# Linear attention plus a gated GLU on one core: interleaved two-sign features, transposes moved to DMA, key-value sums kept in PSUM

## The chip, the cores and the metric

The kernel runs on one core of one Trainium2 chip. The metric is the device time of one execution in microseconds (us), less being better. Spans in the profile run from the first to the last instruction and are 1 to 2 us shorter than the times. The kernel before was run in the same rounds on the same chip each time.

The engines are TensorE (PE in the profile, with PEld for its weight loads), VectorE (DVE), ScalarE (ACT), GpSimd (POOL) and SyncE (SP), which issues most of the DMA transfers. A q after an engine's name (SPq, DVEq) means its queue issuing, not working. PSUM is the memory that TensorE writes its results to; the program uses it as eight banks of 512 columns.

## The reference, cut to what matters

```python
B, S, D, H, Dh, F = 1, 2048, 512, 32, 16, 1792
xn  = layernorm(x)
q, k, v = split(xn @ wqkv)                       # 32 heads of 16
pq, pk  = q @ w_phi, k @ w_phi                   # 16x16 per head
phi_q = concat([softmax(pq), softmax(-pq)])      # 32 features per head
phi_k = concat([softmax(pk), softmax(-pk)])
kv  = einsum("sf,sd->fd", phi_k, v);  z = phi_k.sum(s)      # per head
o   = (phi_q @ kv) / (phi_q @ z + 1e-6)
out = x + o @ wo + ((xn @ w_gate) * (xn @ w_up)) @ w_down
```

Inputs and outputs are bfloat16. There are 16 tiles of 128 tokens.

## The kernel before

`w_phi` is folded into the key and query weights at the start. Each of the 16 token tiles then passes a key stage; after the key-value sums, a query stage. The positive and the negative features lie in two separate tiles. The parts that the change touches are these (all cut).

The loads: all of x, then the attention weights, then the rest, each as one large transfer.

```python
for g in range(4):
    sc.dma(SP, <x tiles 4g..4g+3>, ...)
for w in range(2):
    sc.dma(SP, wqk_v[:, w, :, :], ...)           # query, then key weights
sc.dma(SP, wv_v, ...); sc.dma(SP, wo_v, ...); sc.dma(SP, wg_v, ...); ...
```

The key-value sums come after all key tiles, with a column of ones beside each group of eight heads (129 columns):

```python
for g in range(8):
    pairs = [(ek_v[:, side, t, c*128:(c+1)*128], vext_all[:, t, c, :]) for t in range(NT)]
    mm_group(bank(b, lo, 129), pairs)
```

In the query stage TensorE transposes the features (eight 128x128 blocks per tile), makes numerators (128 columns, most of them masked to zero) and denominators (8 columns) with separate matmuls, and transposes the output (four blocks). ScalarE empties each transpose from PSUM.

```python
for side in range(2):
    items = [(bank(tb[side], c*128, 128), src[:, c*128:(c+1)*128], ident) for c in range(NQ)]
    mm_multi(items)
    act_op(eT_all[:, r, side*4:(side+1)*4, :], bank(tb[side])..., func=ACTF.Copy)
for c in range(NQ): mm_group(bank(bo, c*128, 128), <2 pairs with kvbd>)
for c in range(NQ): mm_group(bank(tb[0], c*8, 8),  <2 pairs with zbd>)
...
mm_multi(<4 transposes of oring>); act_op(oT_v[...], ...)
```

The GLU is done in two ways: 5 of the 14 feature tiles early, in units of 512 tokens; 9 late, in halves of 256 columns, inside the output stage. The residual x is added on TensorE, by a matmul of x with the identity (`acc_mm(i, ident, x_tile(t))`).

The softmax here doesn't subtract the row's maximum and nothing guards it: scores larger than these inputs give would overflow.

Of the kernel before, what the change touches and what calls it, by code (L numbers as in the profile page):

```python
# [5 lines left out]
BF16 = mybir.dt.bfloat16  # L6
# [4 lines left out]
I32 = mybir.dt.int32  # L11
# [6 lines left out]
DH = 16  # L18
# [4 lines left out]
FT_EARLY = 5  # L23


def _ap_intervals(ap, max_n=64):
    esz = mybir.dt.size(ap.dtype)
    off = ap.offset
    pairs = [tuple(pr) for pr in list(ap.ap)[1:] if pr[1] > 1]
    inner_hi = 0  # L30
    rest = []
    for step, cnt in pairs:
        if step == 1:
            inner_hi = max(inner_hi, cnt - 1)
        else:
            rest.append((step, cnt))
    total = 1
    for step, cnt in rest:
        total *= cnt
    if total > max_n:  # L40
        lo, hi = 0, inner_hi
        for step, cnt in rest:
            if step > 0:
                hi += step * (cnt - 1)
            else:
                lo += step * (cnt - 1)
        return [((off + lo) * esz, (off + hi + 1) * esz)]
    outs = []
    for n in range(total):
        base = off  # L50
        m = n
        for step, cnt in rest:
            base += step * (m % cnt)
            m //= cnt
        outs.append((base * esz, (base + inner_hi + 1) * esz))
    return outs


class _Step:
# [3 lines left out]
    def __init__(self, eng, fn, idx, lane):  # L63
        self.eng = eng
        self.fn = fn
        self.idx = idx
        self.deps = []
        self.sig = False
        self.lane = lane
        self.semval = None  # L70
        self.known = {}
        self.waits = []
        self.is_out = False
        self.cost = 100.0
        self.seq = 0
        self.finish = 0.0


class _Sched:

    def __init__(self, nc):
        self.nc = nc
        self.steps = []
        self.by_eng = {PE: [], ACT: [], DVE: [], POOL: [], SP: []}
        self.regions = {}
        self.dma_count = 0
        self.allow_overwrite = False

    def _overlaps(self, space, lo, hi):
        out = []  # L90
        for reg in self.regions.setdefault(space, []):
            if reg[0] < hi and lo < reg[1]:
                out.append(reg)
        return out

    def _record(self, st, reads, writes):
        deps = []
        for ap in reads:
            space = str(ap.tensor.name)
            ivs = _ap_intervals(ap)  # L100
            if space == "ps":
                ivs = sorted(set((lo // 2048 * 2048, (hi + 2047) // 2048 * 2048) for lo, hi in ivs))
            for lo, hi in ivs:
                regs = self._overlaps(space, lo, hi)
                for reg in regs:
                    if reg[2] is not None and reg[2] is not st:
                        deps.append(reg[2])
                    reg[3].append(st)
                if not regs:
                    self.regions[space].append([lo, hi, None, [st]])  # L110
        for ap in writes:
            space = str(ap.tensor.name)
            for lo, hi in _ap_intervals(ap):
                new_regions = []
                for reg in self._overlaps(space, lo, hi):
                    if reg[2] is not None and reg[2] is not st and not reg[3] and not self.allow_overwrite:
                        raise RuntimeError(
                            f"step {st.idx} ({st.eng}) overwrites unread data in {space}[{reg[0]}:{reg[1]}] "
                            f"written by step {reg[2].idx} ({reg[2].eng})")
                    if reg[2] is not None and reg[2] is not st:  # L120
                        deps.append(reg[2])
                    for r in reg[3]:
                        if r is not st:
                            deps.append(r)
                    if reg[0] < lo:
                        new_regions.append([reg[0], lo, reg[2], list(reg[3])])
                    if reg[1] > hi:
                        new_regions.append([hi, reg[1], reg[2], list(reg[3])])
                    self.regions[space].remove(reg)
                self.regions[space].extend(new_regions)  # L130
                self.regions[space].append([lo, hi, st, []])
        seen = set()
        dd = []
        for d in deps:
            if id(d) not in seen:
                seen.add(id(d))
                dd.append(d)
        st.deps = dd

    def step(self, eng, fn, reads=(), writes=(), cost=None):  # L140
        st = _Step(eng, fn, len(self.steps), eng)
        self.steps.append(st)
        self.by_eng[eng].append(st)
        reads = list(reads)
        writes = list(writes)
        self._record(st, reads, writes)
        if cost is None:
            n = 1
            for ap in writes + reads:
                try:  # L150
                    n = max(n, ap.free_size())
                except Exception:
                    pass
            if eng == ACT:
                cost = 230.0 + 0.84 * n
            elif eng == DVE:
                cost = 130.0 + 1.0 * n
            elif eng == POOL:
                cost = 250.0 + 2.2 * n
            else:  # L160
                cost = 100.0 + 0.45 * n
        st.cost = cost
        return st

    def dma(self, eng, out_ap, in_ap, is_out=False, reads=None, writes=None):
        nc = self.nc
        lane = ("dma", self.dma_count)
        self.dma_count += 1
        holder = {}

        def fn(e):
            ins = e.dma_start(out_ap, in_ap)
            return ins

        st = _Step(eng, fn, len(self.steps), lane)
        st.sig = True
        try:
            nbytes = out_ap.free_size() * 2 * 128
        except Exception:
            nbytes = 131072  # L180
        st.cost = 2000.0 + nbytes / 300.0
        self.steps.append(st)
        self.by_eng[eng].append(st)
        r = list(reads) if reads is not None else ([in_ap] if str(in_ap.tensor.name).startswith(("arena", "ps")) else [])
        w = list(writes) if writes is not None else ([out_ap] if str(out_ap.tensor.name).startswith(("arena", "ps")) else [])
        self._record(st, r, w)
        st.is_out = is_out
        return st

# [18 lines left out]
def _build(nc, es, A_x, A_wqkv, A_w_phi, A_wo, B_w_gate, B_w_up, B_w_down, out):  # L208
# [3 lines left out]
    def alloc(name, nelem_bf16, at=None):  # L212
        if at is not None:
            layout[name] = at
            return at
        off = (cur[0] + 31) // 32 * 32
        layout[name] = off
        cur[0] = off + nelem_bf16
        return off

    alloc("x", NT * 512)
    alloc("xnT", NQ * S_TOK)
    alloc("xn", 4 * 512)
    o_wqk = alloc("wqk", 2 * NQ * 512)
    alloc("wT", 2 * NQ * 512)
# [5 lines left out]
    alloc("wd", NF * 512)  # L231
    alloc("wphi", NQ * 16)
# [3 lines left out]
    alloc("bind8", 8)  # L236
    alloc("vext", NT * NQ * 129)
    o_ek = alloc("ek", 2 * NT * 512)
    alloc("ering", 6 * 512, at=o_wqk)
    alloc("enr", 3 * 512, at=o_wqk + 3072)  # L240
    alloc("eT", 2 * 8 * 128, at=o_wqk + 4608)
    alloc("kvbd", 8 * 128, at=o_wqk + 6656)
    alloc("zbd", 8 * 8, at=o_wqk + 7680)
    alloc("oT", NQ * S_TOK, at=o_ek)
    alloc("oring", 3 * 512)
    alloc("gring", 3 * 512)
    alloc("hring", 3 * 512)
    alloc("hT", FT_EARLY * S_TOK)
    alloc("ostg", 3 * 512)
    alloc("stats", 2 * NT * 8)  # L250
    alloc("mv", 2 * NT * 2)
    alloc("rstd", 2 * NT * 2)
    alloc("sums", 2 * 6 * 64)
    alloc("rs", 2 * 6 * 64)
    alloc("small", 2 * 6 * 64)
    alloc("eps", 2 * 2)
    alloc("lnt", 2 * 3 * NT)
    alloc("zcol", 2 * 8 * 2)
    total_bf16 = (cur[0] + 31) // 32 * 32
    assert total_bf16 * 2 <= 207 * 1024, f"arena too big: {total_bf16*2}"  # L260

    arena_t = es.enter_context(nc.sbuf_tensor("arena", [128, total_bf16], BF16))
    arena = arena_t[:, :]
    psum_t = es.enter_context(nc.psum_tensor("ps", [128, 8 * 512], F32))
    psum = psum_t[:, :]

    def sbv(name, lo, n):
# [3 lines left out]
    def sbf(name, lo_f32, n_f32):  # L271
        off = layout[name]
        return arena[:, off:off + 2 * (lo_f32 + n_f32)].bitcast(F32)[:, lo_f32:lo_f32 + n_f32]

    def bank(b, lo=0, n=512):
        return psum[:, b * 512 + lo: b * 512 + lo + n]

    sc = _Sched(nc)
# [658 lines left out]
```

## Time and profile before

The median was 271.5 us of 3 runs (270.5 to 272.2). Only TensorE is near its limit:

| engine | busy us of 270.5 | share |
|---|---|---|
| TensorE matmuls | 246.2 | 91% |
| VectorE | 156.2 | 58% |
| ScalarE | 128.1 | 47% |
| GpSimd | 53.8 | 20% |

The page's second part cuts the span into 40 slices; a digit is the busy share in tenths. Its PE row and the shares of the chain that ended last, from the page of the kernel before:

```profile
PE   0068999999999999999999999999999999999994
PE 80%; DVE 8%; ACT 3%; DMA 3%; issue 3%; POOL 2%; DVEq 0%; POOLq 0%
```

TensorE is full (9) from the fifth slice to the last but one. So the question for any change is how much time its matmuls need and when they begin. Three pieces of the chain in order of time (start us, us, what) were my sources for the cost of one matmul:

```profile
64.39 10.74 PE ps L309 x49
94.65 7.29 PE ps L309 x103
121.61 1.52 PE ps L309 x24
```

Divided they give 0.219, 0.071 and 0.063 us per matmul.

TensorE's start, from the timeline of the kernel before (start us, us, engine, line, operation, shapes, count, and in brackets the idle time before and its releaser):

```profile
14.89 1.04 PE L323 MATMUL ps<-arena 128*128 128x128 bf16 x8 [14.89 <-POOL arena L450]
16.28 1.07 PE L323 MATMUL ps<-arena 128*128 128x128 bf16 x8 [0.35 <-ACT arena L287]
18.04 1.04 PE L323 MATMUL ps<-arena 128*128 128x128 bf16 x8 [0.69 <-ACT arena L287]
```

TensorE has nothing before 14.89 us. The releaser named is POOL, but the weight load that goes with this matmul waits for the transfer of the qkv weights.

### The profile page before, as it was taken

The numbers are of one execution on the slowest core, as the hardware profiler recorded it, in microseconds if no ns is written. First come the engines' busy times: TensorE is split into PE (matmuls) and PEld (weight loads), VectorE is DVE, ScalarE is ACT, GpSimd is POOL, SyncE is SP. The second block draws the span as 40 slices with busy tenths as digits, with TensorE's granted clock in tenths as the row PEclk, the third lists the DMA queues.
The fourth block names the chain that finished last, engine by engine and source line by source line (L and its number), as shares of the span: only waits on it lengthen the run. The fifth ranks groups of instructions, "written<-read, shape, count | busy, mean of one in ns | idle before, by whom it ended". The sixth has DMA issues, their size and how long they took to land.

```text
span 270.5 us, 4879 instructions
## 1 busy us (share of the span) xinstructions
PE 246.2 (91%) x1902; PEld 156.7 (58%) x1936; DVE 156.2 (58%) x364; ACT 128.1 (47%) x261; POOL 53.8 (20%) x99
## 2 busy tenths in 40 slices
PE   0068999999999999999999999999999999999994
PEld 0046544444444587777567765775766757566661
DVE  3951699989797985787677776542232323313231
ACT  1057898646665704776665755632222313222221
POOL 4560253333442430313112131100000000000000
PEclk9999999999999999999999999999999999999999
DMA  6999300000000000000000001001001010000101
GB/s 198 351 393 381 119 0 1 2 0 0 0 0 2 0 4 2 0 2 0 22 19 2 4 1 41 0 2 39 0 2 39 2 39 0 26 15 2 39 1 39
DMA packets 9446, 12.12 MB, mean 45 GB/s; under 512 B 448, under 2 KB 8400, under 8 KB 9424
## 3 DMA queue, kind: packets, MB, share of 16 engines
q1 hardware_dynamic: 9392, 11.80, 12.6%
q8 instruction: 15, 0.25, 0.4%
q0 software_dynamic: 32, 0.02, 0.1%
q14 instruction: 7, 0.06, 0.1%
HBM read 9.72 MB, written 2.10 MB: 44 GB/s over the span
## 4 chain that ended last, share of the span: by engine, by line
PE 80%; DVE 8%; ACT 3%; DMA 3%; issue 3%; POOL 2%; DVEq 0%; POOLq 0%
PE ps L309 50%; PE ps L654 24%; PE ps L323 7%; ACT arena L287 3%; DMA arena<-in_A_w_phi_dram 3%; DVE arena L499 2%; DVE arena L506 1%; DVE arena L534 1%; DVE arena L504 1%; POOL arena L395 1%; DVE arena L465 1%; DVE arena L576 0%; DVE arena L679 0%; DVE arena L457 0%; POOL arena L449 0%
## 5 line engine op out<-in xcount | busy, mean ns | idle before, releaser
L287 ACT ACTIVATE arena<-ps 128x512 bf16<-128x512 f32 (+1 forms) x260 | 126.9, 541 | 138.9 <-PE ps L309 92.9
L309 PE MATMUL ps<-arena 128*128 128x256 bf16 (+4 forms) x1300 | 172.6, 279 | 1.6 <-ACT arena L287 0.5
L309 PEld LDWEIGHTS ps<-arena 128*128 128x128 bf16 x1312 | 109.0, 98 | 59.0 <-PE ps L309 2.2
L654 PE MATMUL ps<-arena 128*128 128x512 bf16 x282 | 77.9, 381 | 2.0 <-DVE arena L679 0.6
L679 DVE TENSOR_TENSOR arena<-ps,arena 128x256 bf16<-128x256 f32 x72 | 30.0, 416 | 55.3 <-PE ps L654 52.9
L323 PE MATMUL ps<-arena 128*128 128x128 bf16 x320 | 30.9, 240 | 17.6 <-POOL arena L450 14.9
L654 PEld LDWEIGHTS ps<-arena 128*128 128x128 bf16 x304 | 28.0, 97 | 24.4 <-PE ps L654 4.4
L323 PEld LDWEIGHTS ps<-arena 128*128 128x128 bf16 x320 | 24.4, 107 | 27.1 <-DMA arena<-in_A_wqkv_dram 14.9
L506 POOL TENSOR_TENSOR arena<-arena 128x512 bf16<-128x512 bf16 x16 | 22.6, 1413 | 34.6 <-DVE arena L504 26.3
L584 POOL TENSOR_TENSOR arena<-arena 128x512 bf16<-128x512 bf16 x16 | 16.9, 1056 | 63.0 <-DVE arena L582 47.0
L576 DVE TENSOR_REDUCE arena<-arena 128x32 f32<-128x512 bf16 x32 | 20.6, 678 | 7.3 <-ACT arena L287 7.2
L499 DVE TENSOR_REDUCE arena<-arena 128x32 f32<-128x512 bf16 x32 | 20.6, 678 | 6.0 <-ACT arena L287 6.0
L534 DVE TENSOR_TENSOR arena<-ps,arena 128x512 bf16<-128x512 f32 x20 | 13.6, 682 | 1.5 <-PE ps L309 1.4
L432 DVE BATCH_NORM_STATS2 arena<-arena 128x6 f32<-128x512 bf16 x16 | 10.5, 684 | 4.8 <-DMA arena<-in_A_x_dram 4.8
L707 DVE CAST arena<-ps 128x512 bf16<-128x512 f32 x8 | 5.5, 692 | 12.4 <-PE ps L654 12.3
L506 DVE TENSOR_TENSOR arena<-arena 128x512 bf16<-128x512 bf16 x16 | 11.6, 728 | 0.4
L465 DVE TENSOR_SCALAR arena<-arena 128x512 bf16<-128x512 bf16 x16 | 5.8, 410 | 9.8 <-PE ps L323 9.8
L621 DVE TENSOR_TENSOR arena<-ps,arena 128x512 bf16<-128x512 f32 x16 | 10.9, 682 | 0.3
L504 DVE RECIPROCAL arena<-arena 128x64 f32<-128x64 f32 x16 | 8.8, 550 | 0.4
L618 DVE SCALAR_TENSOR_TENSOR arena<-arena,ps 128x32 f32<-128x32 f32 x16 | 3.0, 188 | 10.3 <-PE ps L309 10.1
L620 DVE RECIPROCAL arena<-arena 128x32 f32<-128x32 f32 x16 | 5.6, 351 | 0.4
L581 DVE RECIPROCAL arena<-arena 128x32 f32<-128x32 f32 x16 | 5.6, 348 | 0.4
(31 smaller groups left out, 30.3 us busy)
## 6 DMA issues: line engine op xcount, KB each, us to landing
arena<-in_A_x_dram SPq DMA_DIRECT2D x4, 512.0 KB, 6.6
out_dram<-arena SPq DMA_DIRECT2D x16, 128.0 KB, 1.7
arena<-in_B_w_gate_dram SPq DMA_DIRECT2D x1, 1792.0 KB, 12.0
arena<-in_B_w_up_dram SPq DMA_DIRECT2D x1, 1792.0 KB, 15.2
arena<-in_B_w_down_dram SPq DMA_DIRECT2D x1, 1792.0 KB, 18.1
arena<-in_A_wqkv_dram SPq DMA_DIRECT2D x3, 512.0 KB, 11.2
arena<-in_A_wo_dram SPq DMA_DIRECT2D x1, 512.0 KB, 8.9
arena<-in_A_w_phi_dram POOLq DMA_DIRECT2D x1, 16.0 KB, 7.5
```

The source lines that it names most:

```text
L287: return e.activation(out=out_ap, in_=in_ap, func=func, scale=scale, **kw)
L309: ins = e.matmul(out_ap, lhsT=l, rhs=r, start=(i == 0), stop=(i == n - 1))
L323: ins = e.matmul(o, lhsT=l, rhs=r, start=True, stop=True)
L499: dve(lambda e, side=side: e.tensor_reduce(out=sm[:, side * 32:(side + 1) * 32], in_=ering(slot, side).rearrange("p (h f) -> p h f", f=16) ...
L504: dve(lambda e: e.reciprocal(out=rs, in_=sm), [sm], [rs])
L506: fn = (lambda e, side=side: e.tensor_tensor(out=ek_v[:, side, t, :].rearrange("p (h f) -> p h f", f=16), in0=ering(slot, side).rearrange( ...
L534: dve(lambda e: e.tensor_tensor(out=dest_ap, in0=bank(bu), in1=gring(slot), op=ALU.mult), [bank(bu), gring(slot)], [dest_ap])
L576: dve(lambda e, side=side: e.tensor_reduce(out=sm[:, side * 32:(side + 1) * 32], in_=ering(slot, side).rearrange("p (h f) -> p h f", f=16) ...
L584: pool(lambda e: e.tensor_tensor(out=enr(slot).rearrange("p (h f) -> p h f", f=16), in0=ering(slot, 1).rearrange("p (h f) -> p h f", f=16) ...
L621: dve(lambda e: e.tensor_tensor(out=oring(slot).rearrange("p (h d) -> p h d", d=16), in0=bank(bo).rearrange("p (h d) -> p h d", d=16), in1 ...
L654: return e.matmul(o, lhsT=lhsT, rhs=rhs, start=first, stop=last)
L679: dve(lambda e: e.tensor_tensor(out=h, in0=bank(bu, 256, 256), in1=g, op=ALU.mult), [bank(bu, 256, 256), g], [h])
```

## The change

The intent is to take from TensorE all that is not a product of the model. The program is largely rewritten; the diff below is cut to its core and cuts are marked.

```diff
-    <transposes of q features on PE, evacuated by ACT>          # 8 per tile
+    def q_transpose(t):
+        sc.dma(SP, lambda e: e.dma_start_transpose(ph_tile(t), src), ...)       # 256 KB
-    <transposes of o on PE, evacuated by ACT>                   # 4 per tile
+        sc.dma(SP, lambda e: e.dma_start_transpose(oT_tile(t), o_tile(t)), ...) # 128 KB
...
+    # features token-major [token, head, sign, 16]: 4 heads = 128 columns with both signs
+    e_v = sb(name, s*1024, 1024).rearrange("p (h k f) -> p h k f", h=H, k=2)
+    act(e_v[:, :, 0, :], src, func=Exp); act(e_v[:, :, 1, :], src, func=Exp, scale=-1.0)
...
+    # v is scaled by 1/sum; column 17 of each head is 1/sum itself: z comes with kv
+    def kv_acc(t):                       # two tiles after the features, into PSUM banks 0 and 1
+        for c in range(8):
+            e.matmul(bank(c//4, (c%4)*68, 68), lhsT=ek[:, c*128:(c+1)*128], rhs=vs[:, c*68:(c+1)*68],
+                     start=(t == 0 and c % 4 == 0), stop=(t == NT-1))
-    <8 numerator matmuls of 128 columns, 8 denominator matmuls of 8 columns per tile>
+    <8 matmuls of 68 columns per tile: 4 heads x (16 numerators + 1 denominator)>
...
-    <GLU: 5 feature tiles in 512 columns, 9 in 256 columns>
+    <GLU: all 14 feature tiles in 512 columns, spread over the key and query stages>
-    acc_mm(i, ident, x_tile(t))                          # residual on PE
+    dve(lambda e: e.tensor_tensor(out=stg, in0=bank(b), in1=x_tile(t), op=ALU.add), ...)
...
-    <loads: x, query, key, value, wo, gate, up, down>
+    <loads: x 0-1, key, x 2-3, value, gate/up in slices of 256 columns mixed with the rest of x, ...>
-    <1/sqrt of the layernorm by Newton steps on POOL>
+    <by Ln and Exp on ACT>
```

## The prediction

> **What bounds the kernel now.** TensorE. In the busy table PE is busy 246.2 of 270.5 us, in the forty slices it is at 9 from the third to the last, and 80% of the chain that ended last is PE. A sum of issue spacings, read from the timeline, reproduces the span: 644 matmuls of 512 columns at 0.219 us (49 in 10.74 us) = 141; 576 of 256 columns at 0.111 = 64; 576 small ones of 128 or 8 columns at about 0.064 = 37; 128 of 129 columns at 0.071 = 9. Together 251 us. PE starts at 14.9 us (it waits for the qkv weights, loaded after all of x) and the output tail takes 3 us: 269.
>
> **What the change removes, adds, moves.**
> - The 256-column GLU halves become 512-column units: 64 us become 63.
> - Removed from PE: 128 q-feature and 64 output transposes (12 us), 128 denominator matmuls (8 us; the denominator is now column 17 of each head), 16 residual matmuls (3.5 us). Key-value sums and numerators use 68 columns instead of 129 and 128: about 1 us, as weight loads hold these near 0.064.
> - After: 928 matmuls of 512 columns = 203 us, 384 small ones = 25 us: 228, that is 23 us less, all on the critical path because PE is saturated.
> - ACT loses the evacuations of these transposes and of v (64 ops of 0.6 us). DVE gains the v multiply and 8 more residual ops, loses the ek multiply (0.73x16).
> - Start: the key weights are second in the queue, so PE should begin near 6 us. Transposing and folding them is paced by ACT evacuations (0.6 us each, 12 of them), so PE is dense from about 13.5 us, having done 3 of the 228 us. Before, it was dense only near 24 us, having done about 6.
> - Moved to DMA: 32 transposing copies, 256 and 128 KB per token tile, on the queue of SP. No trace here shows one. The Trainium skill, "Advanced Engine Details and Errata", X-Bar Transpose (TRN2), says they run as fast as ordinary ones, about 350-400 GB/s. Then a tile needs 1 us of transfer plus fixed latency, with a lead of three tiles (a tile of the query stage takes 8.8 us of PE with GLU units, 5.3 without). That is hidden.
>
> **New costs.** In the first six key iterations DVE has about 6.3 us (two layernorm tiles 2.3, reduction 1.2, reciprocal 0.55, multiplies 2.2) against PE 6.3 us, with only two PSUM banks for features, v and x transposes: I expect 4 us of PE gaps there and at the boundaries.
>
> **Sum.** 13.5 + 225 + 4 + 3.2 = 246 us; 8 in 10 between 238 and 264. Chances: faster by over 2% 0.86, within 2% 0.05, slower 0.09.
>
> **What would show it.** PE busy near 228; first dense PE at 12 to 15 us; transposing DMAs landing in under 5 us; in the query stage no PE wait on a DMA; gaps of PE in 14 to 55 us released by DVE or ACT; 512-column matmuls still spaced 0.219.
>
> **What would make it wrong.** Slow transposing DMAs. The skill's page "VectorE: DVE Perf Modes", The three transpose paths, gives 1309 ns for one 128x128 block; if that is a rate and not a latency, twelve blocks take 16 us per tile, the query stage is bound by DMA and the kernel is slower than before. The first eight are also chained by completion waits on SP. Second: DVE queue order in the key stage starving the two shared banks, 10 us more.

The 1 us of transfer per tile in it is an estimate worked out from the rate of the page that it names; no run measured that rate.

## The result, and the profile after

The changed kernel took 237.8 us (median of 4 runs, 237.4 to 239.4); the kernel before 271.7 us in the same rounds. The ratio of the fast runs is 0.876, 95% interval 0.871 to 0.880. The forecast, 246 us with a range of 238 to 264, had the direction right and was too cautious: the result lies just below the range.

The lines of the page after that answer to those of before:

```profile
PE   0897959999999999999999999999999999999994
PE 88%; SPq 4%; DVE 3%; DMA 3%; issue 1%
```

TensorE begins earlier, is not full in slices 4 and 6, and is then full to the last but one. The pieces of the chain in the query stage after (line 206 is all 512-column matmuls, line 454 the numerators of 68 columns):

```profile
199.98 3.45 PE ps L206 x16
203.43 0.26 PE ps L454 x8
203.69 4.75 PE ps L206 x22
```

These pieces hold one shape each, so they may be divided: 0.216 us per 512-column matmul and 0.0325 us per 68-column one. The second number is half of what the prediction had charged.

**The cost of a matmul, measured properly.** Taking the start of each single matmul from the recorded trace, and the median distance to the next start after 30 us, gives:

```
columns          8     68    128    129    256    512
ns to the next   25    31.5   56     56    109    216      (before: 8, 128, 129, 256, 512; after: 68, 128, 512)
```

This agrees with the Trainium skill, "TensorE: Matmul & The Clock Gate", Wait — 56ns, not 53.3ns?, which gives N/2.4 GHz plus about 2.5 ns and a floor near 25 ns. The distance is set by the columns, although every matmul here has its own weight load of about 98 ns (the mean of PEld's large groups, both kernels). The loads overlap the matmuls and each other: around the eight 68-column matmuls at 203.27 us they start 30 to 35 ns apart and take 95 to 101 ns each.

**The ledger of the gain.** With these distances the work of TensorE is (the counts are of the program; 34 of 1,936 matmuls are missing from the trace of before, as its weight loads show):

| columns | before | us | after | us |
|---|---|---|---|---|
| 512 | 656 | 141.7 | 928 | 200.4 |
| 256 | 576 | 62.8 | 0 | 0 |
| 128, 129 | 576 | 32.3 | 128 | 7.2 |
| 68 | 0 | 0 | 256 | 8.1 |
| 8 | 128 | 3.2 | 0 | 0 |
| sum | | 240.0 | | 215.7 |

The spans went from 270.5 to 235.7 us, 34.8 us less. Of that, 24.3 us are matmul work. TensorE's first matmul comes 9.2 us earlier (5.7 against 14.9). The rest, idle and slow time of TensorE and the tail, is almost the same in both (about 1 us less).

**What is left at the start.** The timeline of TensorE after, a selection:

```profile
5.72 1.04 PE L309 MATMUL ps<-arena 128*128 128x128 bf16 x8 [5.72 <-POOL arena L287]
...
14.46 3.75 PE L206 MATMUL ps<-arena 128*128 128x512 bf16 x10 [0.22 <-issue]
19.73 0.40 PE L356 MATMUL ps<-arena 128*128 128x128 bf16 x4 [1.52 <-DVE arena L346]
19.97 1.89 PE L206 MATMUL ps<-arena 128*128 128x512 bf16 x8
...
32.66 0.40 PE L356 MATMUL ps<-arena 128*128 128x128 bf16 x4 [2.36 <-DVE arena L346]
32.90 2.75 PE L206 MATMUL ps<-arena 128*128 128x512 bf16 x12
```

Two losses show. Two gaps, before 19.73 and 32.66 us, end when VectorE has normalised a tile of x (line 346). And ten matmuls of 512 columns took 3.75 us at 14.46, though eight took 1.89 us at 19.97. Start to start, the first group is 427 ns apart until 17.4 us, about twice the 216 ns (the shown durations have a tail of some 0.17 us at the end of a group). This is the half rate of a TensorE that has not been busy for long enough (same page, Part 1: The HAM clock gate; it gives some 3.4 us of sustained activity). The trace agrees where TensorE has no pause: in the run with 120 idle matmuls (experiment 7) they are 107 ns apart from 1.85 us on and 56 ns apart from 5.03 us, 3.2 us later. In the control's trace TensorE's idle and slow time, over the distances of the table, is about 11 us between first and last matmul, all of it before 33 us; after that no matmul waits.

The copies that replaced the transposes land 3.1 us after issue (median of 32) and no wait of TensorE on them is in the list of waits.

### The profile page after: what moved, and what is told of

Same layout as the page of the kernel before. It is cut to its first block, busy times and chain, and to the rows that moved or that the text cites. A ratio compares the mean times of both kernels' runs of the same rounds, so it can differ in the third digit from the quotient of the medians.

```text
span 235.7 us, 3357 instructions
## 1 busy us (share of the span) xinstructions
PE 220.7 (94%) x1287; PEld 107.6 (46%) x1312; DVE 146.1 (62%) x282; ACT 87.4 (37%) x165; POOL 42.8 (18%) x65
## 4 chain that ended last, share of the span: by engine, by line
PE 88%; SPq 4%; DVE 3%; DMA 3%; issue 1%
PE ps L206 82%; SPq L238 3%; DMA arena<-in_A_x_dram 3%; PE ps L454 2%; PE ps L413 2%; PE ps L356 1%; DVE arena L337 1%; DVE arena L488 1%; SPq L227 1%; DVE arena L382 0%; PE ps L309 0%; PE ps L320 0%; DVE arena L378 0%; DVE arena L503 0%; DVE arena L346 0%
## 5 line engine op out<-in xcount | busy, mean ns | idle before, releaser
L206 PE MATMUL ps<-arena 128*128 128x512 bf16 x903 | 206.6, 381 | 1.5 <-issue 0.2
L206 PEld LDWEIGHTS ps<-arena 128*128 128x128 bf16 x928 | 88.3, 98 | 100.7 <-issue 2.4
L187 ACT ACTIVATE arena<-ps 128x512 bf16<-128x512 f32 (+1 forms) x152 | 84.5, 597 | 117.2 <-PE ps L206 103.3
L378 DVE TENSOR_REDUCE arena<-arena 128x64 f32<-128x1024 bf16 x32 | 38.9, 1216 | 32.8 <-ACT arena L187 32.8
L388 POOL TENSOR_TENSOR arena<-arena 128x512 bf16<-128x512 bf16 x32 | 34.0, 1061 | 90.6 <-DVE arena L386 86.1
L488 DVE TENSOR_TENSOR arena<-ps,arena 128x512 bf16<-128x512 f32 x56 | 38.4, 686 | 11.9 <-PE ps L206 11.7
L503 DVE TENSOR_TENSOR arena<-ps,arena 128x512 bf16<-128x512 f32 x16 | 11.1, 691 | 30.0 <-PE ps L206 30.0
L400 POOL CAST arena<-arena 128x32 bf16<-128x32 f32 x16 | 5.2, 326 | 77.5 <-DVE arena L382 74.1
L466 DVE TENSOR_TENSOR arena<-ps,arena 128x512 bf16<-128x512 f32 x16 | 11.1, 692 | 0.6
L356 PE MATMUL ps<-arena 128*128 128x128 bf16 x64 | 7.0, 240 | 4.3 <-DVE arena L346 3.9
L401 DVE TENSOR_TENSOR arena<-ps,arena 128x512 bf16<-128x512 f32 x16 | 10.2, 635 | 0.1
L309 PE MATMUL ps<-arena 128*128 128x128 bf16 x32 | 3.8, 264 | 6.0 <-POOL arena L287 5.7
L356 PEld LDWEIGHTS ps<-arena 128*128 128x128 bf16 x64 | 4.9, 105 | 8.6 <-DVE arena L346 4.9
L454 PEld LDWEIGHTS ps<-arena 128*128 128x128 bf16 x128 | 6.2, 97 | 3.8
L413 PEld LDWEIGHTS ps<-arena 128*128 128x128 bf16 x128 | 5.8, 97 | 1.9
L454 PE MATMUL ps<-arena 128*128 128x68 bf16 x128 | 6.7, 194 | 0.0
L413 PE MATMUL ps<-arena 128*128 128x68 bf16 x128 | 6.7, 194 | 0.0
L309 PEld LDWEIGHTS ps<-arena 128*128 128x128 bf16 x32 | 2.7, 117 | 7.4 <-DMA arena<-in_A_wqkv_dram 5.7
L386 DVE TENSOR_TENSOR arena<-arena 128x32 f32<-128x32 f32 x32 | 5.9, 184 | 0.2
## 6 DMA issues: line engine op xcount, KB each, us to landing
arena<-in_A_wo_dram SPq DMA_DIRECT2D x1, 512.0 KB, 11.6
```

Source lines behind the costliest of these rows:

```text
L187: return sc.step(ACT, lambda e: e.activation(out=out_ap, in_=in_ap, func=func, scale=scale, **kw), reads, writes, 130.0 + 0.833 * n)
L206: ins = e.matmul(out_ap, lhsT=l, rhs=r, start=start and i == 0, stop=stop and i == npair - 1, **kw)
L356: ins = e.transpose(bank16(b, q * 128, 128), xn_tile(t)[:, q * 128:(q + 1) * 128], ident)
L378: dve(lambda e: e.tensor_reduce(out=sm, in_=e_v, axis=AX.X, op=ALU.add), [(name, s, 0), (name, s, 1)], [("sums", sr)], 1024)
L388: pool(lambda e: e.tensor_tensor(out=e_v[:, :, 1, :], in0=e_v[:, :, 1, :], in1=rat[:, :, None].to_broadcast([128, H, 16]), op=ALU.mult), [ ...
L401: dve(lambda e: e.tensor_tensor(out=vs_tile(t)[:, :, 0:16], in0=bank(b).rearrange("p (h f) -> p h f", h=H), in1=rp.unsqueeze(2).to_broadca ...
```

## The experiments

There were 17 runs besides the first. They ask whether the terms of the ledger are real (1 to 4), whether the copies through DMA are free (5), and what the early start is worth (6 and 7). Everywhere below the ratio is to the kernel before of the same rounds. The changed kernel itself, repeated as a control, gave 0.877 (237.7 us) and in the last set, on another chip, 0.880 (239.0 us).

### 1. Control

No edit.

> The changed kernel unaltered, as the control of this set. All theories: 237 to 239 us. Spacing of its 256 matmuls of 68 columns, start to start, again about 31 ns.

Measured: 237.67 us, ratio 0.877, span 235.7 us. Spans here and below are those of the profiled execution. The 256 matmuls of 68 columns are again 31.5 ns apart.

### 2. Columns or weight loads

```diff
-            ins = e.matmul(bank(c // 4, (c % 4) * CW, CW), ..., rhs=vs[:, c * CW:(c + 1) * CW], ...)
+            ins = e.matmul(bank(c // 4, (c % 4) * 128, 128), ..., rhs=vs[:, c * CW:c * CW + 128], ...)
```

The numerators likewise; the outputs are stored 128 columns apart and the extra 60 are ignored.

> The 256 key-value and numerator matmuls stream 128 columns (68 useful, 60 ignored) instead of 68. Theory W (the recorded prediction: weight loads hold a small matmul near 64 ns, whatever its columns): spacing and time unchanged, within 1 us. Theory C (columns set the spacing[...]): spacing goes from 31 to 56 ns, 256 x 0.025 = 6.3 us longer, about 244 us.

Measured: 244.8 us, ratio 0.902, span 242.1 us, which is 6.4 us over the control's. The spacing rose to 56 ns. The same place of the timeline in the control, then in this run (columns as above):

```profile
203.29 0.42 PE L454 MATMUL ps<-arena 128*128 128x68 bf16 x8
203.54 2.75 PE L206 MATMUL ps<-arena 128*128 128x512 bf16 x12
```

```profile
203.55 0.61 PE L462 MATMUL ps<-arena 128*128 128x128 bf16 x8
204.00 2.32 PE L208 MATMUL ps<-arena 128*128 128x512 bf16 x10
```

From the start of the eight to the start of what follows it is 0.25 us against 0.45. Theory C holds and the prediction's claim about weight loads falls. Packing numerator and denominator into 68 columns is worth all of its columns.

### 3. The transposes back on TensorE

```diff
-        sc.dma(SP, lambda e: e.dma_start_transpose(ph_tile(t), src), ...)
+        <8 e.transpose into a PSUM bank>; act(ph_tile(t), <bank>, ...)
-        sc.dma(SP, lambda e: e.dma_start_transpose(oT_tile(t), o_tile(t)), ...)
+        <4 e.transpose into the same bank>; act(oT_tile(t), <bank>, ...)
```

> Both transposes of the query stage go back to TensorE (192 transposing matmuls of 128 columns), evacuated by ScalarE. Theory C: TensorE is without gaps there, so the time grows by 192 x 0.056 = 10.8 us, to about 248.5 us. The recorded prediction (64 ns each) says 12.3 us. Rival: the transposes fall into gaps that the copies through DMA had left, or ScalarE's 32 more evacuations make new waits: growth under 6 us or over 15 us.

Measured: 262.2 us, ratio 0.966, span 258.6 us: 22.9 us over the control, far more than the 10.7 us of matmuls. The gaps have a name, in the timeline of this run:

```profile
211.97 0.61 PE L445 MATMUL ps<-arena 128*128 128x128 bf16 x8
212.51 0.42 PE L462 MATMUL ps<-arena 128*128 128x68 bf16 x8
214.32 0.40 PE L485 MATMUL ps<-arena 128*128 128x128 bf16 x4 [1.39 <-ACT arena L187]
```

The transposes of the output (485) wait for ScalarE to empty the bank that the feature transposes (445) had filled. My placement made that wait, so a second version gives them separate banks once the GLU units, which hold four of the eight banks, are done:

```diff
-        b = 2 if ups else 3        # o_transpose
+        b = 2 if ups else 7
-        b = 3 if ups else 4 + i % 4
+        b = 3 if ups else 4 + i % 3
```

> As e_petr, but once the GLU units are done the two transposes use separate PSUM banks (3 and 7) and the output tiles three banks. e_petr grew by 22.9 us of span: 10.7 us of matmuls and 12.3 us of TensorE gaps, 8.9 of them after 190 us, where an output transpose waits for ScalarE to empty the same bank. Theory (the transposes themselves cost only their 10.7 us, the rest was bank sharing): span about 250 us, time about 252 us. Rival (ScalarE's 32 evacuations are themselves the limit): no change from e_petr's 262 us.

Measured: 254.5 us, ratio 0.936, span 252.9 us, 17.2 us over the control. TensorE's gaps after 190 us fell from 8.9 to about 1 us, as the theory said. Those at 119 to 144 us (3.5 us), where the GLU units still hold their banks, stayed. Some 2 us of the 17.2 are not the transposes': this execution fell to half rate from 20.1 to 23.5 us, after a gap at the start that the control has too. The one run at full granted clock has a span of 251.0 us, 15.3 over the control's and 1 us over the forecast. So moving the transposes to DMA saves 10.7 us of matmuls, and in this schedule also waits for PSUM banks and ScalarE's emptying, another 4.6 us. How many of those a third placement would recover is open.

### 4. The residual back on TensorE

```diff
-        mm(bank(b), [(oT_tile(t)[:, q, :], wo_v[:, q, :]) for q in range(NQ)], ...)
+        mm(bank(b), [(oT_tile(t)[:, q, :], wo_v[:, q, :]) for q in range(NQ)] + [(ident, x_tile(t))], ...)
-        dve(lambda e: e.tensor_tensor(out=stg, in0=bank(b), in1=x_tile(t), op=ALU.add), ...)
+        dve(lambda e: e.tensor_copy(out=stg, in_=bank(b)), ...)
```

> The residual goes back to TensorE: 16 more matmuls of 512 columns against the identity, VectorE only copies out. Theory (TensorE saturated to the last tile): 16 x 0.216 = 3.5 us longer, about 241.3 us. Rival (the output evacuations or stores set the pace at the end): under 1 us.

Measured: 242.1 us, ratio 0.892, span 239.8 us, 4.1 us over the control. 16 matmuls at 0.216 us are 3.5 us of it; the gaps before 33 us differed by the rest. VectorE reads the bank in either case and takes the same 0.69 us for adding as for copying (lines 503 and 504 of the two pages), so the residual there is free.

### 5. Every transposing copy twice

```diff
         sc.dma(SP, lambda e: e.dma_start_transpose(ph_tile(t), src), ...)
+        sc.dma(SP, lambda e: e.dma_start_transpose(spare, src), ...)
         sc.dma(SP, lambda e: e.dma_start_transpose(oT_tile(t), o_tile(t)), ...)
+        sc.dma(SP, lambda e: e.dma_start_transpose(spare, o_tile(t)), ...)
```

> Each of the 32 transposing copies is issued twice, the second into a spare tile that nobody reads. Theory (the copies are hidden behind TensorE): within 1 us of 237.7, and twice as many transposing packets in the trace. Rival (the copies or the SP queue that issues them are near the limit): over 3 us longer, with TensorE waiting for DMA in the query stage.

Measured: 244.3 us, ratio 0.900: 6.6 us slower, so they are not free without limit. TensorE lost 5.1 us near 217 to 226 us: two gaps, and half rate for a while after the first. They end when VectorE has made the output tile (line 469), which itself waited 11.6 us in all for copies:

```profile
219.86 0.61 PE L457 MATMUL ps<-arena 128*128 128x68 bf16 x8 [2.69 <-DVE arena L469]
```

The queue of SP in the changed kernel, then here, from the timeline (SPq is the issuing itself):

```profile
203.32 0.33 SPq L505 DMA_DIRECT2D out_dram<-arena  x1
203.70 1.24 SPq L440 DMA_TRANSPOSE arena<-arena  x1
205.05 1.21 SPq L470 DMA_TRANSPOSE arena<-arena  x1
208.33 0.33 SPq L505 DMA_DIRECT2D out_dram<-arena  x1
```

```profile
202.72 0.58 SPq L510 DMA_DIRECT2D out_dram<-arena  x1
203.34 1.24 SPq L441 DMA_TRANSPOSE arena<-arena  x1
204.62 1.27 SPq L473 DMA_TRANSPOSE arena<-arena  x1
205.94 1.31 SPq L443 DMA_TRANSPOSE arena<-arena  x1
207.29 0.58 SPq L510 DMA_DIRECT2D out_dram<-arena  x1
```

Each transposing copy holds SP for 1.2 to 1.3 us, whatever its size of the two here. The changed kernel issues two and a store in 2.8 of the 5.0 us that TensorE needs per tile. Doubled, they need about 5.7 us, and SP runs without a pause. But this run also had waits of one copy for another (17.9 us on SP in total, lines 443 and 475, from the shared spare tile), so a second version doubles only the feature copies and gives them two spare tiles.

> Only the 16 feature copies (256 KB) are issued twice. In e_dbl the SP queue ran without a pause near 203 to 219 us, 5.7 us per tile (four copies of 1.27 us to issue and one store) against 5.0 us of TensorE. Here it needs about 4.2 us per tile. Theory I (the issue time of SP is the limit that e_dbl hit): hidden again, within 1.5 us of 237.7. Rival T (the transfers themselves, or the waits for a copy before, set the limit): at least half of e_dbl's 6.5 us stays, 241 us or more.

Measured: 238.5 us, ratio 0.879 against the control's 0.877: within the noise. With 1.67 times the transposed bytes and three copies per tile the cost is hidden again. This fits the issue time of SP as the limit. The rate of the transfers is not it: from 200 to 210 us this run moved 170 GB/s without holding up TensorE, the first version only 149. It does not clear the waits between the copies of the first version, which this one removed as well.

### 6. The order of the loads

Only the loads are put back to before's order (with the key weights ahead of the query weights):

```diff
-    load_x(0, 2); load_qk(SP, 1); load_x(2, 2); <v, slices of gate/up and the rest of x mixed>
+    for t0 in range(0, NT, 4): load_x(t0, 4)
+    load_qk(SP, 1); load_qk(SP, 0); <v>; for s in range(FF // FSL): load_gu(SP, s)
```

> Only the order of the loads is put back: all of x, then key, query and value weights, then gate and up. Theory (the early key weights buy the start): TensorE begins near 14.5 instead of 5.7 us, and since the tiles of x are then early the two gaps of 4.5 us in all after 17 us may close: 5 to 9 us longer, 243 to 247 us. Rival (VectorE and ScalarE set the pace of the start): under 2 us.

Measured: 237.8 us, ratio 0.877: no difference at all, which is the rival's number. TensorE began at 10.9 us, 5.1 us later than the control, and its first 512-column matmul came at 18.7 instead of 13.7 us. But it then had no gap: its idle and slow time is about 7 us against 11 us. The early start is real and is given back. With it the tiles of x land later, and in the changed kernel VectorE waits for one of them just before the first gap, until 16.57 us; the trace of this run has no such wait after 13 us:

```profile
16.57 0.69 DVE L337 BATCH_NORM_STATS2 arena<-arena 128x6 f32<-128x512 bf16 x1 [2.29 <-DMA arena<-in_A_x_dram]
```

One thing is left open. Start plus idle and slow time is 27.3 us in the kernel before (14.9 + 12.4), 17.8 here and 16.9 in the changed kernel. So over 9 us were gained there with the old order of loads, by parts that no run tested alone: the key weights ahead of the query weights, the layernorm off GpSimd, the new order of the GLU units.

The converse was tried on the kernel before:

```diff
+    load_x(0); load_qk(1); load_qk(0); <x 1..3>          # was: x 0..3, query, key
```

> The kernel before with one part of the change alone: key and query weights are loaded after the first four tiles of x instead of after all sixteen. Theory: TensorE begins near 7 us instead of 14.9 and the time falls by 6 to 9 us, to 262 to 265 us. Rival (its layernorm chain through POOL and the late mask weights set the start): under 2 us.

Measured: 266.9 us, ratio 0.983 (0.978 to 0.988). TensorE began at 6.0 instead of 14.9 us, yet the time fell by 4 us only, short of the theory's 6 to 9. Here too about half of an early start is lost in later waits.

### 7. What takes the early start back

First, a gate for the layernorm statistics, so that they do not sit in VectorE's queue ahead of what TensorE needs:

```diff
-    load_gu(SP, 1); load_gu(SP, 2); load_x(8, 4)
+    load_x(8, 4); load_gu(SP, 1); load_gu(SP, 2)
-    dve(<bn_stats of tile t>, [("x", t)], ...)
+    dve(<bn_stats of tile t>, [("x", t)] + ([("xnT", t0 - 4)] if t0 >= 8 else []), ...)
```

> Two edits at the start: x tiles 8 to 11 load before the gate and up slices 1 and 2, and the layernorm statistics of tiles 8 to 15 wait until the first tile of the group before is transposed. Theory (VectorE's queue put these statistics, which waited for their load or held the queue, ahead of the layernorm that TensorE waited for): the gaps of 1.85 and 2.74 us close, about 4 us shorter, 233.5 us. Rival (VectorE has too much work there in any order): under 1.5 us, the gaps move.

Measured: 240.2 us, ratio 0.885: slower. Three gaps of 2.4 us instead of two (in this section a gap is from one matmul's start to the next). The rival was closer. It was not statistics directly ahead of it that held the normalising up: before each of the three gaps VectorE was idle for 1.4 to 2.1 us, waiting for ScalarE, and then did three other operations before the normalising (line 347) that TensorE waited for. Around the first gap:

```profile
16.35 1.22 DVE L379 TENSOR_REDUCE arena<-arena 128x64 f32<-128x1024 bf16 x1 [2.06 <-ACT arena L187]
18.54 0.32 DVE L347 TENSOR_SCALAR arena<-arena 128x512 bf16<-128x512 bf16 x1
```

Then the half rate, with idle matmuls on the identity from 1.9 us on:

```diff
+    warm(36)                     # matmuls of 128 columns, ident x ident, into an unused bank
     for jt in range(NQ):
         w_transpose(1, jt)
+        warm(3)
```

and so on after each of the 12 units of the start.

> 36 matmuls of 128 columns on the identity before the first real one and three after each of the 12 units of the start, results unused. Theory (TensorE runs at half rate, 107 and 428 ns per matmul of 128 and 512 columns, until it has been busy for a few us; here until 17.3 us): full rate before the first 512-column matmul, about 2 us shorter, 235.5 us. Rival (the half rate ends by time or cannot be shifted by idle work, or the 2 us are lost again in the gap at 17.9 us): under 0.7 us.

Measured: 240.6 us, ratio 0.888: slower, too. The half rate was gone: the first twelve 512-column matmuls took 2.76 us. But TensorE then met a gap of 6.35 us, and was at half rate after it. Both edits together:

> e_gate and e_warm together. Theory: both gains add, about 6 us shorter than the changed kernel, 231.5 us, and TensorE's idle and slow time falls from 11.5 to about 5 us. Rival: warm TensorE meets the layernorm queue earlier and waits there, 233.5 us or more.

Measured: 238.0 us, ratio 0.879, three gaps of 2.4 us left. No gain over the control.

Since the late loads had shown no gaps, the next kernel keeps the key weights second and brings all of x right after:

```diff
+    load_x(0, 2); load_qk(SP, 1); load_x(2, 2); load_x(4, 4); load_gu(SP, 0)
+    load_x(8, 4); <v>; load_x(12, 4); <the rest>
```

> Only the order of the loads: key weights stay second, but all of x is loaded by 3.5 MB (value weights and gate/up slice 0 mixed in), so that the layernorm statistics of all tiles can run before the key loop. e_late had no gaps but began 5.2 us later; the changed kernel began early and lost 4.6 us in two gaps. Theory (the gaps come from late tiles of x in VectorE's queue): early start and no gaps, 4 to 5 us shorter, 233 us. Rival (an early start always meets VectorE's statistics, as in e_gate): 237 us or more, gaps of over 1.5 us stay.

Measured: 235.5 us, ratio 0.872: the gap near 18 us is gone, the one near 28 us (2.75 us) is not. That is at most half of the theory's gain: 2.1 us by the medians, 1.4 us by the ratios.

The half rate by itself is seen best where there are no gaps:

> e_late with 120 idle matmuls before the first real one and three after each of its 12 start units. e_late has no gaps that could swallow a gain, and runs its first twelve 512-column matmuls at 428 ns until 21 us. Theory (idle work lifts the half rate): they run at 216 ns and the time falls by 2 to 3 us below e_late's 237.8, to about 235.3 us. Rival (e_warm's lesson: the gain of a warm start is lost elsewhere): within 0.7 us of 237.8.

Measured: 235.5 us, ratio 0.870 against 0.877 for the same loads without idle matmuls. Its timeline, with that of the run with late loads alone first:

```profile
18.69 4.66 PE L206 MATMUL ps<-arena 128*128 128x512 bf16 x12 [0.20 <-ACT arena L187]
```

```profile
17.61 2.76 PE L206 MATMUL ps<-arena 128*128 128x512 bf16 x12
```

Twelve matmuls take 2.76 instead of 4.66 us, and the start before them is 1 us shorter. The half rate costs 2 to 3 us, and idle work lifts it.

> e_xall with the 36 idle matmuls and three after each start unit. Theory: full rate from about 5.7 us, first 512-column matmul at 12.6 us, no gap over 1 us, hence 12.6 + 213 + 3.3 + 1 = 230 us. Rival: a gap near 15 us stays, where tile 4 of x must be normalised in time: 233 us or more.

Measured: 233.5 us, ratio 0.864: the rival's number, though the gap near 15 us that it named is closed. The gap of 2.75 us at 25.4 us was left:

```profile
28.14 0.40 PE L356 MATMUL ps<-arena 128*128 128x128 bf16 x4 [2.37 <-DVE arena L346]
```

So the last kernel also makes the statistics in groups of two tiles, one group per key iteration:

```diff
-        if t in (0, 2, 4):
-            ln_stats(4 + 2 * t, 4)
+        if t < 4:
+            ln_stats(8 + 2 * t, 2)      # tiles 4 to 7 in two groups ahead of the loop
```

> best3, with the layernorm statistics in groups of two tiles, one per key iteration, instead of groups of four. In best3 one gap of 2.75 us is left at 25.4 us: the normalising of tile 8 waits until the statistics of tiles 8 to 11 are aggregated, and after it TensorE runs at half rate again for a while. Theory (the group size makes the gap): gap closed, 3 to 4 us shorter than best3, about 230 us. Rival (VectorE simply has too much to do before 30 us): 233 us or more.

Measured: 230.5 us (230.35 to 230.73), ratio 0.850 (0.847 to 0.853), correct. From 13 us on no gap over 0.7 us is left:

```profile
13.06 2.54 PE L206 MATMUL ps<-arena 128*128 128x512 bf16 x11 [0.15 <-ACT arena L187]
15.43 0.39 PE L356 MATMUL ps<-arena 128*128 128x128 bf16 x4
15.65 1.89 PE L206 MATMUL ps<-arena 128*128 128x512 bf16 x8
```

The control of the same rounds:

> The changed kernel again, on the same chip and in the same rounds as best4: 237 to 239 us.

Measured: 239.0 us, ratio 0.880. So the last kernel is 3.4% faster than the changed one (0.850 over 0.880). This control also shows what the runs of 239 us are. Its timeline after the second gap:

```profile
32.65 0.40 PE L356 MATMUL ps<-arena 128*128 128x128 bf16 x4 [2.36 <-DVE arena L346]
32.88 4.44 PE L206 MATMUL ps<-arena 128*128 128x512 bf16 x12
```

The first control has 2.75 us for these twelve. The same gap sends TensorE to half rate for some microseconds in one execution and not in another: about 1.9 us. In this set the four controls of over 238.5 us have a granted clock (the clock that the profile says TensorE had) of 0.993, the two near 237.7 of 1.000. The last kernel has no such gap, and its five runs lie within 0.4 us.

## Why the prediction was right or wrong

It was wrong in its number: 237.8 us, below a range that began at 238. The mechanism was right, and the term that was mis-sized is named first.

- **The work of TensorE after, "228 us", was wrong.** It is 215.7 us. The failing step is "weight loads hold these near 0.064": the 256 matmuls of 68 columns cost 0.0315 us, which is 8.3 us less. Another 3 us come from 0.219 instead of 0.216 us for 928 matmuls, and 1 us from the transposes (0.064 against 0.056). Experiment 2 shows that columns and not weight loads set the spacing.
- **How it was misread.** The 0.064 came from a piece of 24 matmuls in 1.52 us, and these were eight each of 256, 128 and 8 columns (8 x (0.109 + 0.056 + 0.025) = 1.52). The 0.071 came from a row labelled with one shape, 129 columns, that also held 512-column matmuls. The 0.219 came from a row of 49 in which one record is missing.
- **"Reproduces the span" was no proof.** The sum of before was 251 us by these spacings and is 240.0 us. It met the span only because some 12 us of gaps and half rate near the start and after were left out. Two errors cancelled.
- **"23 us less, all on the critical path" was near.** It is 24.3 us, and experiments 2 to 4 show that each part added back costs at least its matmul time.
- **The start, "PE should begin near 6 us", "dense from about 13.5 us", was right**: 5.7 and 13.6 us. That it was worth its 9 us was not tested in the prediction, and experiment 6 shows that in the changed kernel the order of the loads alone is worth nothing.
- **"4 us of PE gaps" was near**: the two gaps are 4.2 us net, and the releaser is VectorE, as forecast. The reason forecast, too much work for VectorE with two PSUM banks, is not what the later runs point to: the order of the loads closed the first gap and smaller groups of statistics the second, with VectorE as busy as before (145.1 us against 146.1). So the size was partly luck. The half rate, about 2 us, was not in the sum.
- **The copies through DMA are hidden, as forecast**: 3.1 us to landing against "under 5 us". "Advanced Engine Details and Errata", X-Bar Transpose (TRN2), which likens their rate to ordinary transfers, was the better guide, in so far as the copies stayed hidden. The likeness itself is not borne out: in experiment 5's second version the DMA engines' share was 0.94 at 170 GB/s (200 to 210 us), while the changed kernel's loads moved 317 GB/s at a share of 1.11 (14 to 33 us). The 1309 ns per block of "VectorE: DVE Perf Modes", The three transpose paths, is not a rate in this case, as twelve blocks took 2.45 us to issue and did not hold up TensorE. What limits them sooner than the rate is SP's issue time, as far as experiment 5 goes.

The new sum for the span is 13.6 us to the first 512-column matmul, 213 us of work left then (215.7 less 48 x 0.056), 6 us of gaps and half rate, and 3.3 us from the last matmul's start to the end: 236, against 235.7 us measured.

## What to carry to other kernels

Cost a matmul from the distance between single starts of one shape, never from a merged row, and do not take a sum that meets the span as proof of its terms. On a saturated TensorE, columns streamed are the currency: drop padding, fold a denominator into spare columns, and move transposes and residuals to engines with room, counting SP's issue time for each copy. An earlier start is worth only what the next engine can follow, so check the first 30 us for gaps released by VectorE and for matmuls at twice their usual distance before moving loads.

## What the Trainium skill lacked or had wrong

- "TensorE: Matmul & The Clock Gate", Back-to-back issue gap, says that in a stream of weight loads and matmuls 128 columns take about 81 ns and 512 about 131 ns, and that the formula N/2.4 + 2.5 is for isolated matmuls. Here, in such streams, the distances are 56 and 216 ns, as the formula has them.
- The same section names about 62 ns per matmul as the bound for small matmuls with hardware decode off. That bound did not hold in these runs, which show 31.5 ns at 68 columns and 25 ns at 8; which way the decode was set is not on record, so this is no contradiction.
- The same page, Part 1, gives an idle window of about 3.4 us before the half rate returns. A gap with 2.36 us of idle TensorE was enough in one of two executions of the changed kernel compared here (twelve matmuls in 4.44 us after it, half rate from 33.3 to 36.7 us; 2.75 us in the other).
- The same page, Seeing it yourself, warns in general that clock events in a trace can be unreliable, but not that the first half rate can be missing: the window from 14 to 33 us reads 1.00 after, while matmuls were 427 ns apart until 17.4 us. The first clock record of this trace is the change to full rate at 17.3 us.
- The pages on DMA give bandwidths for the transposing copy on this chip, but no time that issuing one of this size from SBUF to SBUF takes on it: it held SP for 1.2 to 1.3 us, against 0.33 us for a store, and as far as experiment 5 goes that was nearer its limit than the bytes.
